# Linear attention into hash-routed experts on one Trainium2 core: k of six batches moved to GpSimd's queue, and a new written order of the first phase

## Chip, core and metric

The kernel runs on one core of a Trainium2 chip. The metric is device time in microseconds. The core has five engines with queues of their own: TensorE (PE, with its weight loads as PEld), VectorE (DVE), ScalarE (ACT), GpSimd (POOL) and SyncE (SP). SP and POOL issue the transfers of this kernel; what they issue is carried by 16 DMA engines.

## What is computed

```python
q_s = exp(q - max(q)) / (sum over head_dim + 1e-9)      # softmax of each row of q
k_s = exp(k - max(k)) / (sum over seq + 1e-9)           # softmax of k along the sequence
kv  = einsum('bhsd,bhse->bhde', k_s, v)                 # 64 x 64 per batch and head
x   = einsum('bhsd,bhde->bhse', q_s, kv)                # as rows: 4608 tokens x 512
expert = token_ids * 2654435761 % 8
out[expert == e] = relu(x[expert == e] @ w1[e]) @ w2[e] # w1 512 x 1024, w2 1024 x 512
```

q, k and v are (8 batches, 8 heads, 576 positions, 64), float32. All 4608 tokens go to one of 8 experts.

## The kernel before

The kernel works in float16 and routes first, so that q is read only in the order in which the experts want it. The index part (L79 to L163) counts where each token goes: an expert has 640 slots, 72 for each of the 8 batches and 64 for tokens beyond 72 of a batch (overflow). Slots are handled in five blocks of 128.

**Names of the steps.** The first phase is cut into named steps, and the list `ORDER` says in which sequence their instructions are issued. Each engine gets its instructions in that sequence (`manual_schedule` covers GpSimd, TensorE, VectorE and ScalarE); between engines semaphores hold. The names:

- V*b*: load v of batch b on POOL's queue, float32 to float16 (L725). k is loaded on SP's queue (L721).
- EK*b*: exp of k on ACT (L324). MK*b*: ones into two columns of v on ACT (L328). KV*b*: 72 matmuls k^T v (L338). SC*b*: division by the sums on DVE (L345 to L351), which gives `kvr` of the batch.
- CNT, OVA, OHA, FND, FDD, QS, ROP, ROD: the overflow tokens. FDD ends with their row numbers `oidx`; ROD ends with the rows of the output.
- G*e*: gather of q rows of expert e, five indirect transfers on POOL (L362). GO: four such for the overflow tokens, which need `oidx`.
- EQ*e_i*: exp of block i on ACT (L373). SM*e*a, SM*e*b: sums over head_dim on DVE (L385 to L387). ML*e*a, ML*e*b: the scaling on DVE (L391). TP*e_i*, TC*e_i*: transposition on TensorE (L403) and its copy. O stands for the overflow tokens.
- PP*e_lo r*, PC*e_lo r*: product of q with `kvr` of the batches from lo on, for head pair r (L414), and its copy into `XT` (L826). XP, XC: the same for the overflow tokens (L437, L801). SH, SD, OV: their distribution over the experts (L447, L453, L811).
- W*e*1, W*e*2: load of w1 or w2 of expert e on POOL's queue in two halves, float32 to float16 (L465).
- A*e_lo_f*, R*e_lo_f*: the first layer, 8 matmuls of 128x288 or 128x352 (L479), and its ReLU on ACT (L484). B*e_i*, C*e_i*, S*e_i*: the second layer, 8 matmuls of 128x512 (L491), its scaling on DVE (L497) and the indirect store on POOL (L501).

`ORDER` covers all batches, the gathers of experts 0 to 4, and both layers of experts 0 and 1. After it a loop over experts 2 to 7 follows (40 blocks of L479 and L491 by turns), into which gathers, weights and products for later experts are placed by position.

**Buffers.** k has three buffers, its exp two, v four, q rows ten, the scaled result four, and each weight one of two pools (even and odd experts). In PSUM there are two buffers of each of three kinds. A load waits until the step that last read its buffer is done: W21 for expert 0's first layer, W12 for nothing.

**Queues.** POOL's transfers count on eight semaphores in turn, so each waits for the landing of the eighth before it. Before `ORDER` starts, SP issues the token numbers and k of batches 0 to 2, and POOL v of batches 0 and 1. Then SP issues k of batch b + 3 as a part of step EK*b*:

```python
def expk(b):
    k16s[b] = at.expk(kraws[b], apool)
    if b + 3 < B_:
        load_k(b + 3)
```

SP does nothing else, so that each k leaves as soon as its buffer is free. On POOL the sequence is, from the built program: v0, v1, v2, G0, v3, v4, GO, W01, v5, G1, v6, v7, W02, W11, W12, G2, G3, first stores of expert 0, W21, G4.

Of the kernel before, what the change touches and what calls it, by code (L numbers as in the profile page):

```python
# [17 lines left out]
B_, H_, S_, DH_ = 8, 8, 576, 64  # L18
# [608 lines left out]


ORDER = """
EK0 MK0 V2 CNT KV0 G0 EK1 OVA SC0 MK1 KV1 OHA EK2 V3 V4 SC1 FND MK2 FDD KV2 EK3 QS GO EQ0_1 ROP SC2 EQ0_0 EQ0_2  # L630
EQ0_3 SM0a EQ0_4 EK4 W01 ROD V5 ML0a G1 SM0b TP0_2 TP0_1 TC0_2 TC0_1 TP0_0 MK3 ML0b TC0_0 KV3 TP0_4 SC3 EK5 V6
TP0_3 V7 W02 TC0_4 MK4 W11 PP0_00 TC0_3 KV4 PC0_00 EQO_0 W12 EQO_1 PP0_01 SC4 EK6 PP0_03 SMOa EQO_3 EQO_2 PC0_01
MLOa PP0_02 G2 PC0_02 SMOb TPO_0 TCO_0 TPO_1 PC0_03 XP0 TCO_1 MLOb A0_0_1 XC0 A0_0_3 R0_0_1 TPO_3 R0_0_3 TPO_2
A0_0_0 MK5 EQ1_0 KV5 EQ1_1 R0_0_0 EQ1_4 EQ1_3 A0_0_2 SC5 EK7 XP1 SM1b MK6 ML1b XC1 KV6 R0_0_2 EQ1_2 MK7 G3 SM1a
TCO_3 KV7 TCO_2 ML1a TP1_3 TP1_4 TC1_3 TC1_4 SC6 TP1_2 TP1_1 TC1_2 SC7 TC1_1 XP2 TP1_0 XC2 PP0_40 XP3 TC1_0
PC0_40 B0_0 XC3 PP1_01 C0_0 PP1_41 SH1 PC1_01 S0_0 PC1_41 PP0_42 SD1 PP1_42 SH0 PC1_42 PC0_42 PP0_43 SD0 PP0_41
B0_1 EQ2_0 PC0_41 OV0 EQ2_1 PC0_43 EQ2_2 PP1_02 C0_1 PP1_00 EQ2_3 A0_288_0 SM2a S0_1 PC1_02 EQ3_1 A0_288_2 EQ3_2
ML2a PC1_00 PP1_03 R0_288_2 PP1_43 R0_288_0 A0_288_1 PC1_43 EQ3_3 PC1_03 TP2_2 EQ3_0 OV1 TP2_0 R0_288_1 TC2_2
A1_0_2 TC2_0 EQ3_4 SM3a A0_288_3 R1_0_2 EQ2_4 PP1_40 W21 A1_0_0 R0_288_3 ML3a TP2_1 PC1_40 G4 B0_2 R1_0_0 TC2_1
SM2b A1_288_3 TP3_1 R1_288_3 C0_2 TP3_0 B0_3 ML2b TC3_1 A1_288_0 C0_3 S0_2 TC3_0 TP2_4 SM3b R1_288_0 S0_3 PP2_03  # L640
B0_4 TC2_4 ML3b PP2_02 W22 A1_288_1 PC2_02 PC2_03 TP3_2 C0_4 R1_288_1 TP2_3 A1_0_1 TC3_2 EQ4_3 S0_4 TC2_3 EQ4_4
PP2_01 TP3_3 EQ4_2 PC2_01 A1_0_3 TC3_3 R1_0_1 PP2_00 TP3_4 R1_0_3 A1_288_2 TC3_4 W31 PC2_00 EQ4_0 PP2_61 PP2_60
R1_288_2 PC2_61 B1_0 EQ4_1 PC2_60 PP2_62 C1_0 PP2_30 PC2_62 B1_2 PC2_30 S1_0 PP2_31 C1_2 PP2_32 B1_3 PC2_31
PC2_32 S1_2 PP2_33 C1_3 PP2_63 B1_1 PC2_33 S1_3 PC2_63 B1_4 C1_1 S1_1 C1_4 S1_4
""".split()


class _Steps:
# [5 lines left out]
    def add(self, name, f, *args):  # L654
        assert name not in self.f, name
        self.f[name] = lambda: f(*args)
# [27 lines left out]
def kernel(  # L684
# [10 lines left out]
    nc = tc.nc  # L695
    V, A = nc.vector.tensor_copy, nc.scalar.copy
    fpool = ctx.enter_context(tc.tile_pool(name="flag", bufs=1))
    with ExitStack() as fctx:
# [17 lines left out]
        with tc.manual_schedule(engines={eng.Pool, eng.PE, eng.DVE, eng.Activation}):  # L716
            kraws, v16s, k16s, pkvs, qs, po, pr, ph, obs, wts, px, pq = ({} for _ in range(12))

            def load_k(b):
                kraws[b] = apool.tile([128, NPAIR * C9 * DH_], F32, tag="kraw", name=f"kraw{b}", bufs=3)  # L720
                nc.sync.dma_start(kraws[b][:], k[b])  # L721

            def load_v(b):
                v16s[b] = apool.tile([128, NPAIR * C9, VW], F16, tag="v16", name=f"v16_{b}", bufs=4)
                nc.gpsimd.dma_start(v16s[b][:].rearrange("p c d -> p (c d)"), v[b])  # L725
# [2 lines left out]
            at.clear()  # L728
            ix = _Index(nc, moe_token_ids, cpool, ipool, ps)
            moe = _Moe(nc, tc, moe_w1, moe_w2, out, ix, ps)  # L730
            for b in range(3):
                load_k(b)
            load_v(0)
            load_v(1)
            ix.consts(tpool)
            ix.core(cpool, lambda: at.fill(ix))

# [4 lines left out]
            add = st.add  # L742
# [6 lines left out]

            def expk(b):  # L750
                k16s[b] = at.expk(kraws[b], apool)
                if b + 3 < B_:
                    load_k(b + 3)

            for b in range(B_):
                if b > 1:
                    add(f"V{b}", load_v, b)
                add(f"EK{b}", expk, b)
                add(f"MK{b}", lambda b: at.mark(v16s[b]), b)
                add(f"KV{b}", lambda b: pkvs.update({b: at.keys(k16s[b], v16s[b])}), b)  # L760
                add(f"SC{b}", lambda b: at.scaled(b, pkvs[b], apool), b)
# [195 lines left out]
```

The softmax here doesn't subtract the row's maximum and nothing guards it: scores larger than these inputs give would overflow.

## Time and profile before

| | |
|---|---|
| time, median of 3 | 239.14 us (238.75 to 239.44) |
| span of the profiled execution (239.44 us) | 237.7 us |
| busy: PE / DVE / ACT / POOL | 196.2 / 138.2 / 113.3 / 116.9 us |
| HBM read / written | 63.25 / 10.49 MB |
| first matmul of expert 0's first layer | 54.6 us |
| start of the loop over experts 2 to 7 | 116.7 us |
| last matmul | 231.4 us |

Times count from the first instruction of the profiled execution. A matmul is pipelined, so PE busy tells that it had work and not how fast it went; for that one divides a group's length by its matmuls. In the chain of waits each step leads to what released the next one, from the start to the last instruction: what stands there with many microseconds was waited for, and by whom is the next line. A group of instructions is given with its line, its output and inputs and its tile sizes.

### The profile page before, as it was taken

To read this page: it belongs to the slowest core of one execution; us is meant where nothing else is said; L and a number is where in the kernel's file an instruction comes from. 1 tells how busy PE (TensorE), PEld (TensorE's weight loads), DVE (VectorE), ACT (ScalarE), POOL (GpSimd) and SP (SyncE) were. 2 spreads that over 40 slices of the span, in tenths; PEclk is the share of its full clock that TensorE was granted. 3 is DMA by queue.
4 is the path that set the end of the run, shared out by engine and by line. 5 is a ranking of instruction groups with operands and counts; after the bars stand their busy time and mean duration, and the time that the engine had idled before them with its cause. 6 is when DMAs were issued, how large, how long until landed. Compare 5 with 4: busy or idle time off the path is not lost.

```text
span 237.7 us, 4865 instructions
## 1 busy us (share of the span) xinstructions
PE 196.2 (83%) x1955; PEld 128.7 (54%) x1955; DVE 138.2 (58%) x260; ACT 113.3 (48%) x175; POOL 116.9 (49%) x140
## 2 busy tenths in 40 slices
PE   3535624629779989999979999999999999999990
PEld 2435623616665556575556476567457656647530
DVE  7995639292592699963387395679358561131140
ACT  8633337764954495284154354555525324405400
POOL 6072332535263545775358788558762254053061
PEclk9999999855955999999999999999999999999996
DMA  6999999999999944969937999997999598832032
GB/s 216 331 311 320 411 337 277 351 227 295 213 215 223 308 165 63 261 168 225 249 112 184 241 228 284 210 243 195 208 226 266 128 204 160 164 133 86 1 130 84
DMA packets 13549, 51.42 MB, mean 216 GB/s; under 512 B 2505, under 2 KB 2505, under 8 KB 12497
## 3 DMA queue, kind: packets, MB, share of 16 engines
q0 software_dynamic: 12224, 41.58, 72.2%
q1 hardware_dynamic: 1296, 9.47, 10.1%
q8 instruction: 17, 0.28, 0.5%
q14 instruction: 12, 0.09, 0.1%
HBM read 63.25 MB, written 10.49 MB: 310 GB/s over the span
## 4 chain that ended last, share of the span: by engine, by line
PE 55%; DMA 24%; DVE 9%; issue 4%; ACT 4%; POOL 2%; POOLq 0%; DVEq 0%; ACTq 0%
PE po L491 24%; PE ph L479 23%; DMA raw<-in_q_dram,gidx 14%; DMA v<-in_v_dram 5%; DMA out_dram<-ob,sidx 4%; PE pq L403 3%; DVE rq L385 2%; ACT k L324 2%; PE px L426 2%; POOL raw L362 2%; PE pt L338 2%; DVE qs L391 1%; DVE A L127 1%; DMA ids<-in_moe_token_ids_dram 1%; ACT qs L373 1%
## 5 line engine op out<-in xcount | busy, mean ns | idle before, releaser
L479 PE MATMUL ph<-XT,w1r 128*128 128x320 f16 (+2 forms) x512 | 76.0, 304 | 0.4 <-ACT hT L484 0.4
L491 PE MATMUL po<-w2r,hT 128*128 128x512 f16 x320 | 74.3, 384 | 0.0
L484 ACT ACTIVATE hT<-ph 128x640 f16<-128x640 f32 (+2 forms) x64 | 44.9, 704 | 51.1 <-PE ph L479 50.8
L501 POOL DMA_INDIRECT out_dram<-ob,sidx x40 | 40.8, 1020 | 56.4 <-DVE ob L497 51.6
L497 DVE TENSOR_SCALAR ob<-po 128x512 f32<-128x512 f32 x40 | 27.6, 690 | 62.4 <-PE po L491 54.9
L362 POOL DMA_INDIRECT raw<-in_q_dram,gidx x40 | 46.7, 1169 | 30.6 <-DVE row L162 6.6
L479 PEld LDWEIGHTS <-w1r 128*128 128x128 f16 x512 | 50.0, 100 | 21.1 <-issue 0.9
L491 PEld LDWEIGHTS <-hT 128*128 128x128 f16 x320 | 30.9, 99 | 34.0 <-issue 1.8
L373 ACT ACTIVATE qs<-raw 128x512 f16<-128x512 f32 (+1 forms) x44 | 26.0, 625 | 17.3 <-DMA raw<-in_q_dram,gidx 17.1
L385 DVE TENSOR_REDUCE rq<-qs 128x16 f32<-128x1024 f16 (+1 forms) x18 | 26.1, 1450 | 4.4 <-ACT qs L373 4.3
L403 PE MATMUL pq<-ident,qs 128*128 128x128 f16 (+1 forms) x176 | 16.7, 237 | 12.0 <-DVE qs L391 11.0
L391 DVE TENSOR_TENSOR qs<-qs,rq 128x1024 f16<-128x1024 f16 (+1 forms) x18 | 26.2, 1455 | 0.3
L338 PE MATMUL pt<-v,k 64*64 64x65 f16 x576 | 15.4, 226 | 10.3 <-ACT v L328 8.9
L403 PEld LDWEIGHTS <-qs 128*128 128x128 f16 (+1 forms) x176 | 12.7, 108 | 16.6 <-issue 9.7
L338 PEld LDWEIGHTS <-k 64*64 64x64 f16 x576 | 15.0, 139 | 10.9 <-issue 10.4
L324 ACT ACTIVATE k<-kraw 128x2304 f16<-128x2304 f32 x8 | 16.9, 2118 | 1.9 <-PE pt L338 1.5
L465 POOL DMA_DIRECT2D w1r<-in_moe_w_dram x16 | 9.3, 580 | 9.1 <-PE px L414 6.1
L414 PE MATMUL px<-qT,kvr 128*128 128x72 f16 (+1 forms) x96 | 8.0, 215 | 5.4 <-DVE XT L826 3.0
L414 PEld LDWEIGHTS <-kvr 128*128 128x128 f16 x96 | 6.3, 103 | 8.5 <-issue 6.0
L877 ACT CAST XT<-px 128x864 f16<-128x864 f32 (+1 forms) x6 | 4.8, 799 | 11.9 <-PE px L426 11.9
L465 POOL DMA_DIRECT2D w2r<-in_moe_w_dram x16 | 9.4, 594 | 2.1 <-DMA v<-in_v_dram 1.6
L345 DVE TENSOR_SCALAR rec<-pt 128x4 f32<-128x4 f32 x8 | 1.3, 162 | 15.2 <-PE pt L338 15.1
(106 smaller groups left out, 136.4 us busy)
## 6 DMA issues: line engine op xcount, KB each, us to landing
kraw<-in_k_dram SPq DMA_DIRECT2D x8, 1152.0 KB, 10.3
w1r<-in_moe_w_dram POOLq DMA_DIRECT2D x16, 512.0 KB, 8.5
w2r<-in_moe_w_dram POOLq DMA_DIRECT2D x16, 512.0 KB, 8.5
v<-in_v_dram POOLq DMA_DIRECT2D x8, 594.0 KB, 16.3
raw<-in_q_dram,gidx POOLq DMA_INDIRECT x40, 6.2
out_dram<-ob,sidx POOLq DMA_INDIRECT x40, 6.8
raw<-in_q_dram,oidx POOLq DMA_INDIRECT x4, 15.5
ids<-in_moe_token_ids_dram SPq DMA_DIRECT2D x1, 36.0 KB, 1.9
```

What stands on the lines that cost most here:

```text
L324: self.nc.scalar.activation(k16[:].rearrange("p c d -> p (c d)"), kraw[:], ACT.Exp)
L338: nc.tensor.matmul(pkv[s, r, 0:DH_ + 1], lhsT=k16[s, r * C9 + c, :], rhs=v16[s, r * C9 + c, 0:DH_ + 1], start=(c == 0), stop=(c == C9 - 1))
L362: nc.gpsimd.indirect_dma_start(out=raw[0:w, :], out_offset=None, in_=self.q[:, :], in_offset=bass.IndirectOffsetOnAxis(ap=idx[0:w, i:i + 1 ...
L373: self.nc.scalar.activation(q16[0:w, i].rearrange("p h d -> p (h d)"), raws[i][0:w, :], ACT.Exp)
L385: nc.vector.reduce_sum(rv, qv, axis=AX.X)
L391: nc.vector.tensor_tensor(out=qf, in0=qf, in1=rv.rearrange("p i h -> p (i h)").unsqueeze(2) .to_broadcast([w, (hi - lo) * H_, DH_]), op=AL ...
L403: nc.tensor.transpose(pv[:, r, o:o + w[j]], q16[0:w[j], j, 2 * r:2 * r + 2, :] .rearrange("p h d -> p (h d)"), self.ident[0:w[j], 0:w[j]])
L479: nc.tensor.matmul(ph[:, i, :hi - lo], lhsT=w1r[:, dc, fc * 128:(fc + 1) * 128], rhs=XTp[:, e % 2, dc, lo:hi], start=(dc == 0), stop=(dc = ...
L484: self.nc.scalar.activation(hT[:, 2 * f2:2 * f2 + 2, lo:hi], ph[:, :, :hi - lo], ACT.Relu)
L491: nc.tensor.matmul(po[:], lhsT=hT[:, fc, blk * 128:(blk + 1) * 128], rhs=w2r[:, fc, :], start=(fc == 0), stop=(fc == FC - 1))
L497: self.nc.vector.tensor_scalar(out=ob[:], in0=po[:], scalar1=1.0 / SX, scalar2=None, op0=ALU.mult)
L501: sc = self.nc.gpsimd.indirect_dma_start(out=self.out[:, :], out_offset=bass.IndirectOffsetOnAxis(ap=self.ix.sidx[:, e, blk:blk + 1], axis=0),
```

## The change

k of batches 0 and 1 stay on SP. k of batch 2 is issued on POOL after v0 and v1, and k of batches 3 to 7 become steps K3 to K7 of `ORDER`, on POOL too. `ORDER` is replaced as a whole: the same steps in another sequence. POOL's transfers are then, from the built program: v0, v1, k2, G0, k3, G1, v2, v5, GO, k4, v3, v4, k6, k5, v6, k7, v7, G2, W01, G4, W11, G3, W02, W21, W12, six stores, W31, W22. On TensorE, expert 0's first layer (A0) comes after the last KV and after the overflow's SH, where it stood between them before; A0, A1, B0 and B1 follow one another with TP2, TP3 and PP2 among them. The loop over experts 2 to 7 is as it was.

```diff
             def load_k(b):
                 kraws[b] = apool.tile([128, NPAIR * C9 * DH_], F32, tag="kraw", name=f"kraw{b}", bufs=3)
-                nc.sync.dma_start(kraws[b][:], k[b])
+                (nc.sync if b < 2 else nc.gpsimd).dma_start(kraws[b][:], k[b])
...
-            for b in range(3):
+            for b in range(2):
                 load_k(b)
-            load_v(0)
-            load_v(1)
+            for b in range(2):
+                load_v(b)
+            load_k(2)
...
             def expk(b):
                 k16s[b] = at.expk(kraws[b], apool)
-                if b + 3 < B_:
-                    load_k(b + 3)

             for b in range(B_):
                 if b > 1:
                     add(f"V{b}", load_v, b)
+                if b > 2:
+                    add(f"K{b}", load_k, b)
```

`ORDER` before, up to the first layer of expert 1, and after, up to the second layer of expert 0:

```diff
-EK0 MK0 V2 CNT KV0 G0 EK1 OVA SC0 MK1 KV1 OHA EK2 V3 V4 SC1 FND MK2 FDD KV2 EK3 QS GO EQ0_1 ROP SC2 EQ0_0 EQ0_2
-EQ0_3 SM0a EQ0_4 EK4 W01 ROD V5 ML0a G1 SM0b TP0_2 TP0_1 TC0_2 TC0_1 TP0_0 MK3 ML0b TC0_0 KV3 TP0_4 SC3 EK5 V6
-TP0_3 V7 W02 TC0_4 MK4 W11 PP0_00 TC0_3 KV4 PC0_00 EQO_0 W12 EQO_1 PP0_01 SC4 EK6 PP0_03 SMOa EQO_3 EQO_2 PC0_01
-MLOa PP0_02 G2 PC0_02 SMOb TPO_0 TCO_0 TPO_1 PC0_03 XP0 TCO_1 MLOb A0_0_1 XC0 A0_0_3 R0_0_1 TPO_3 R0_0_3 TPO_2
-A0_0_0 MK5 EQ1_0 KV5 EQ1_1 R0_0_0 EQ1_4 EQ1_3 A0_0_2 SC5 EK7 XP1 SM1b MK6 ML1b XC1 KV6 R0_0_2 EQ1_2 MK7 G3 SM1a
-TCO_3 KV7 TCO_2 ML1a TP1_3 TP1_4 TC1_3 TC1_4 SC6 TP1_2 TP1_1 TC1_2 SC7 TC1_1 XP2 TP1_0 XC2 PP0_40 XP3 TC1_0
...
+EK0 CNT G0 EK1 MK0 OVA KV0 MK1 KV1 SC0 K3 OHA G1 EK2 SC1 FND EQ0_0 EQ0_3 EQ0_1 EQ0_2 FDD EQ0_4 SM0a EK3 V2 V5 GO
+QS EQ1_0 EQ1_2 ML0a ROP EQ1_4 EQ1_3 SM0b EQ1_1 TP0_0 TP0_2 TC0_0 TC0_2 TP0_1 ROD MK2 K4 TC0_1 KV2 ML0b V3 V4
+SM1a K6 MK5 TP0_4 TP0_3 TC0_4 K5 EQO_0 V6 EQO_1 ML1a EQO_2 TC0_3 EQO_3 SMOa TP1_0 TP1_2 TC1_0 TC1_2 TP1_1 EK4
+SMOb MLOa TC1_1 K7 MK3 MLOb TPO_0 KV3 TCO_0 SM1b TPO_2 V7 TPO_1 TCO_2 MK4 G2 SC3 TPO_3 TCO_1 TCO_3 ML1b XP0 XC0
+SC2 TP1_3 KV4 TC1_3 PP1_01 PP0_01 SC4 EK6 XP1 PC0_01 W01 PC1_01 PP0_03 XC1 PC0_03 PP1_00 G4 EK5 PP1_02 PC1_02
+KV5 PC1_00 MK6 KV6 SC5 EK7 PP0_00 PP1_03 SC6 XP2 W11 PC0_00 PC1_03 MK7 PP0_02 XC2 KV7 PC0_02 TP1_4 SC7 EQ2_0
+EQ2_4 PP0_43 EQ2_2 XP3 PC0_43 XC3 PP0_42 EQ2_1 SH0 PC0_42 SM2a EQ2_3 TC1_4 PP0_41 G3 SH1 PC0_41 SD0 PP1_41
+PP0_40 SD1 A0_0_0 ML2a PC0_40 A0_0_3 R0_0_0 PP1_43 A0_0_1 R0_0_3 OV0 PC1_43 A0_0_2 R0_0_1 OV1 W02 PP1_40 SM2b
...
```

More of the change, by code (lines that the diff above doesn't have):

```diff
@@ L635 @@
-TCO_3 KV7 TCO_2 ML1a TP1_3 TP1_4 TC1_3 TC1_4 SC6 TP1_2 TP1_1 TC1_2 SC7 TC1_1 XP2 TP1_0 XC2 PP0_40 XP3 TC1_0
[L636 to L644, printed above, removed]
+EK0 CNT G0 EK1 MK0 OVA KV0 MK1 KV1 SC0 K3 OHA G1 EK2 SC1 FND EQ0_0 EQ0_3 EQ0_1 EQ0_2 FDD EQ0_4 SM0a EK3 V2 V5 GO
@@ new lines @@
+EQ2_4 PP0_43 EQ2_2 XP3 PC0_43 XC3 PP0_42 EQ2_1 SH0 PC0_42 SM2a EQ2_3 TC1_4 PP0_41 G3 SH1 PC0_41 SD0 PP1_41
+PP0_40 SD1 A0_0_0 ML2a PC0_40 A0_0_3 R0_0_0 PP1_43 A0_0_1 R0_0_3 OV0 PC1_43 A0_0_2 R0_0_1 OV1 W02 PP1_40 SM2b
+A0_288_3 R0_0_2 PC1_40 A0_288_2 R0_288_3 PC1_41 ML2b EQ3_0 TP2_1 A1_0_2 R0_288_2 TC2_1 TP2_3 EQ3_2 A1_0_3 TC2_3
+R1_0_2 PP1_42 TP2_4 EQ3_1 A0_288_0 TC2_4 R1_0_3 SM3a PC1_42 TP2_0 A0_288_1 R0_288_0 EQ3_3 A1_288_2 W21 TC2_0
+R0_288_1 ML3a TP2_2 EQ3_4 B0_3 W12 EQ4_2 EQ4_0 SM3b TP3_2 EQ4_1 B0_1 EQ4_3 TC3_2 EQ4_4 ML3b TP3_1 R1_288_2
@@ L645 @@
+A1_288_1 TC3_1 C0_1 TP3_3 R1_288_1 A1_288_3 TC3_3 S0_1 C0_3 B0_2 TC2_2 R1_288_3 S0_3 PP2_30 C0_2 PP2_32 PC2_30
+B0_0 PC2_32 S0_2 PP2_33 C0_0 PP2_31 A1_0_0 PC2_33 S0_0 PC2_31 A1_0_1 R1_0_0 TP3_0 TP3_4 R1_0_1 TC3_0 B0_4 TC3_4
+PP2_02 C0_4 PP2_62 PC2_02 B1_0 PC2_62 S0_4 PP2_01 C1_0 PP2_00 A1_288_0 PC2_00 PC2_01 S1_0 PP2_61 PP2_03 R1_288_0
+PC2_61 B1_1 W31 PC2_03 W22 B1_2 C1_1 S1_1 B1_4 C1_2 S1_2 B1_3 C1_4 S1_4 PP2_60 PP2_63 C1_3 PC2_60 PC2_63 S1_3
 """.split()
```

## The prediction

> **What bounds the kernel now.** I read the busy slices first, then a table of busy time by stage, then the chain of waits, and last the timelines of TensorE and GpSimd around the places that the chain names.
>
> The slices: each digit is the busy tenth of 5.94 us.
> ```profile
> PE   3535624629779989999979999999999999999990
> PEclk9999999855955999999999999999999999999996
> DMA  6999999999999944969937999997999598832032
> ...
> HBM read 63.25 MB, written 10.49 MB: 310 GB/s over the span
> ```
> DMA is full in the first 14 slices (83 us) while TensorE has holes; then TensorE is full and DMA has holes. So there are two phases, and only the first has time to give. The stage table (stage, its length, busy of PE, PEld, DVE, ACT, POOL, then granted clock, DMA share, GB/s landed) puts numbers on it:
> ```profile
> 0.00:54.00 54.00, 23.87 (x567) 21.77 (x567) 37.09 (x102) 30.89 (x40) 22.01 (x40) 0.92 0.99 310
> 54.00:88.20 34.20, 30.54 (x409) 20.27 (x409) 20.41 (x38) 21.85 (x42) 15.90 (x19) 0.77 0.97 241
> 88.20:116.70 28.50, 28.45 (x213) 17.56 (x213) 20.65 (x38) 13.54 (x25) 17.11 (x18) 1.00 0.79 174
> ...
> 116.70:231.40 114.70, 113.29 (x769) 69.10 (x767) 59.34 (x84) 47.05 (x69) 60.70 (x64) 1.00 0.75 183
> ```
> From 88.2 us TensorE idles 1.5 us in all; the loop over experts 2 to 7 (from 116.7) is 114.7 us of matmuls. The loop is not edited. So the question is when the loop starts.
>
> The chain, before the dense part (start, length, what):
> ```profile
> 16.99 19.84 DMA raw<-in_q_dram,gidx
> ...
> 53.55 10.94 DMA v<-in_v_dram
> ...
> 67.69 14.12 DMA raw<-in_q_dram,gidx
> ...
> 89.00 2.17 PE ph L479 x16
> ```
> Three transfers that stood behind others in a full DMA. TensorE itself (start, length, group, idle before):
> ```profile
> 54.61 4.02 PE L479 MATMUL ph<-XT,w1r 128*128 128x288 f16 x16
> ...
> 60.39 1.34 PE L338 MATMUL pt<-v,k 64*64 64x65 f16 x72
> 61.67 1.15 PE L479 MATMUL ph<-XT,w1r 128*128 128x288 f16 x8
> ...
> 64.39 1.34 PE L338 MATMUL pt<-v,k 64*64 64x65 f16 x72 [1.22 <-ACT v L328]
> 66.08 2.14 PE L338 MATMUL pt<-v,k 64*64 64x65 f16 x72 [0.35 <-ACT v L328]
> ...
> 88.83 2.34 PE L479 MATMUL ph<-XT,w1r 128*128 128x288 f16 x16
> ```
> Expert 0 starts at 54.6, before batches 5 to 7 have arrived, and crawls among them: 251 ns per matmul at 54.6, 146 ns at 88.8. The last batches come at 64 to 66 because W01, G1 and, on SP, all of k share the DMA with v.
>
> **What the Trainium skill says.** "DMA: Bandwidth & Descriptors", section "Issuing engines are not separate DMA queues": transfers of SP, ACT and GpSimd run on the same 16 engines. The trace agrees: the DMA share is 1.03 at 20 to 40 us with both queues and 1.03 at 60 to 83 us, after the last k, with GpSimd's alone. Moving k there buys order, not bandwidth. The same page, "Queues, rings and completion order": an engine takes packets from its queues in turn. The trace agrees that two queues delay each other: of the loads issued at the start the quickest k lands in 5.3 us, no v in under 10.9. "TensorE: Matmul & The Clock Gate", section "What's actually happening": an idle array runs at half clock until some 3.4 us of sustained work. The pairs above (251 and 146 ns; 2.14 and 1.34 us) agree. The granted-clock row says 9 before 44 us, yet a batch of L338 takes 2.19 us there; I go by the durations.
>
> **The change, part by part.** Bytes are from the tile shapes at 4 bytes read per element: k 1.18 MB a batch, v 1.217, a gather of five (G) 1.18, GO 1.05, half an expert's weights (W) 2.10. For the whole kernel they give 9.44 + 9.73 + 10.49 + 33.55 = 63.2 MB, the page's 63.25. By the landing of the last v (53.55 + 10.94 = 64.5) all k and v, G0, G1, GO and W01 had been read in queue order, 24.7 MB in 62.5 us from 2.0: **395 GB/s**.
>
> *The order of transfers.* After: k0, k1, v0, v1, k2, G0, k3, G1, v2, v5, GO, k4, v3, v4, k6, k5, v6, k7, v7, G2, W01, G4, W11, G3, W02, W21, W12. Up to v7 this is 22.6 MB: 57.2 us of DMA. A gap must be added. Gathers follow each other every 1.3 us (13.05, 14.39, 15.69, 16.99), 0.262 MB each, 202 GB/s, half the rate; before, SP's k filled the other half. G1 is issued at about 19 to 26 with a backlog that ends near 23, and v2 follows: 2 us lost, bounds 0 (backlog covers it) and 8 (all nine gathers of G1 and GO at half rate, 11.7 us for 5.6 us of data, 6.1, and 2 for GO waiting for its indices). So v7 lands at 2.0 + 57.2 + 2 = 61.2, W01 at 69.5, W11 at 77.8, W02 at 86.
>
> *k on GpSimd's queue* adds six DMA issues of 0.57 us (the v row), 3.4 us, while GpSimd was busy 38 of 88 us: hidden. Behind a waiting k now stand v and gathers. k7 waits for EK4 on ACT, EK4 for TP1 and so for ML1a. VectorE's work up to ML1a ends at about 37 by its rows; k7 is issued near 42, when DMA has transfers queued to 55: nothing. v7 waits for KV3, which stands behind TPO_0 and MLOa (about 42): issued at 45, nothing. GO waits for the overflow indices (25.2 before; about 24 after, since v1 comes earlier), queue position 27: nothing. W21 waits for expert 0's first layer, with W12 behind it; W02 is still moving then.
>
> *The chain after v7.* MK7 0.3, KV7 2.1 (cold), SC7 1.25 (0.16 + 0.18 + 0.86 and gaps): 64.9. TensorE then has two overflow products and shares (16 matmuls of L447: 3.5 us warm, 216 ns as in L491; 6.7 cold, as the eight of L491 at 73.5 us took 3.35) and five small groups, 1.0 to 1.8 us: A0_0_0 starts at 69.4 (warm) to 73.4 (cold). W01 lands at 69.5, no later than that. I take the middle, **71.4**; A0 starts 17 us later than now.
>
> *From there to the loop*, by warm rows of the chain: A0 and A1 are each 4 x 0.98 + 4 x 1.19 = 8.7 us; B0 and B1 5 x 1.73 = 8.65; TP2 and TP3 ten of 0.22, 2.2; PP2 4 x (0.19 + 0.19 + 0.13), 2.0; three PP1 of 0.13, 0.4. Sum 39.3 us. Before, 62 us pass from the first A0 block to the loop. Waits: W11 at 77.8 is needed at about 79, W02 at 86 at about 86, W12 near 97 at about 102. For those two, and 1.7 of lost clock at half odds, I add 1.9. In these 41 us ACT has 16 ReLUs of 0.7, ten exponentials of 0.6 and some ten evictions of 0.45, 22 us; VectorE two softmaxes of 6.8 (1.75, 1.76, 1.21, 1.21 and the small ones) and ten each of 0.42, 0.69 and 0.5, 30 us: hidden. The loop starts at 71.4 + 39.3 + 1.9 = 112.6 instead of 116.7: **4.1 us earlier**. Everything behind it is the same instructions. The sum is against the profiled span of 237.7; that execution took 239.44, the three 238.75 to 239.44. I take the difference off the median: 239.14 - 4.1 = 235.0.
>
> **Rivals.**
> *Warm and full (229).* DMA runs at 416 GB/s without a gap (33.3 MB from 2 to 83 us, less than the waits allow) and TensorE stays warm: W01 at 64.2 sets A0, W02 at 80 makes B0 wait 2, loop at 64.2 + 39.3 + 2 + 1 = 106.5, 10 us gained. For it: the stretch before v7 has TensorE work for most of its time. Against it: the cold rows up to 54 us at a similar load.
> *Gathers starve the queue (slower, 241).* Place: G1 and GO, 19 to 33 us. Price: 8 us of DMA instead of 2; v7 and A0 6 us later, loop at 118.6, +1.9: 241.0. It decides from 4 us above my 2. For it: the 1.3 us spacing. Against it: k3, v2 and v5 stand among the gathers.
> *Given back (239).* The loop starts earlier, but W22, issued only after B1_0, lands late: A0 to B1_0 is 30 us, so issue near 104, landing near 115 with W31; it is needed at 112.6 + 8.7 = 121. Against it: 6 us of slack.
>
> **How the numbers follow.** A measurement of this kernel tells about 0.3% from no change. Likeliest 0.50 (232 to 238); warm and full 0.22; starved 0.20; given back 0.08. The own range of the likeliest takes A0 at 69.4 to 73.4 and waits of 1 to 3. The range 228.5 to 240.5 takes in the second case and most of the third. Faster: 0.50 + 0.22 and 0.02 of the fourth, 0.74. Same: 0.05 of the fourth and 0.03 of the third, 0.08. Slower: 0.18.
>
> **What would show it.** Right: DMA at 9 until about 90 us; MK7 near 61; first L479 matmul at 69 to 74 and no hole over 1 us after it; the loop near 113. Warm: L447 at 216 ns, not 420. Starved: a DMA slice under 9 between 19 and 35 us. Given back: PE waiting on L491 for w2r at 121. Wrong altogether: the loop starting at 117 or later with v7 landed by 61.

## The result, and the profile after

| | before | after |
|---|---|---|
| time, median of 4 runs | 239.08 us (238.75 to 239.44) | 235.27 us (234.83 to 235.74) |
| span of the profiled execution | 237.7 us | 234.0 us |
| MK7, the first step that needs v7 | 65.8 us | 63.7 us |
| first matmul of expert 0's first layer (A0) | 54.6 us | 74.2 us |
| start of the loop over experts 2 to 7 | 116.7 us | 114.0 us |
| last matmul | 231.4 us | 228.0 us |

The ratio is 0.984, with a 95% interval of 0.982 to 0.987. The forecast was 235.0 us. Later runs of the same kernel on another chip gave another sign; they stand under the experiments and belong to the result. Runs far above the fastest of their kernel count as slow, and every ratio given compares fast runs alone while the medians are of all runs, so that the two can differ (1.029 against 1.022 in after_again) and in before_ob6 even point opposite ways (1.004 against 0.992).

The busy slices of the kernel after, each digit 5.85 us:

```profile
PE   3554345383789999999999999999989999999990
PEclk9998555587668999999999999999999999999998
DMA  6999899999999989946999999998999598832032
...
HBM read 63.25 MB, written 10.49 MB: 315 GB/s over the span
```

DMA holds 8 or more from the second slice to the 17th (6 to 99 us); the 8 in slice 5 (23 to 29 us) stands where the gathers of G1 and GO are issued. TensorE is full from slice 13 (70 us).

The table of stages (start and end, length, busy of PE, PEld, DVE, ACT and POOL, granted clock, DMA share, GB/s landed), the first three rows for the stages shown of before, the last for the loop:

```profile
0.00:54.00 54.00, 26.45 (x599) 23.15 (x600) 44.83 (x110) 34.70 (x51) 31.71 (x48) 0.75 0.96 293
54.00:88.20 34.20, 29.02 (x418) 20.95 (x418) 19.86 (x41) 22.62 (x40) 16.59 (x21) 0.80 0.98 256
88.20:116.70 28.50, 28.50 (x193) 16.64 (x192) 16.48 (x29) 10.60 (x19) 13.70 (x17) 1.00 0.84 179
114.00:228.00 114.00, 113.29 (x771) 69.19 (x768) 59.76 (x85) 47.34 (x70) 60.88 (x64) 1.00 0.80 191
```

VectorE's busy time up to 54 us rose from 37.1 to 44.8 us and ACT's from 30.9 to 34.7: softmaxes and copies have moved in front, into time in which TensorE waited for k and v anyway. TensorE's busy time in the loop stands at 113.29 us in both kernels.

The chain of waits of the kernel after (start, length, what):

```profile
48.37 15.32 DMA v<-in_v_dram
...
64.50 1.53 PE pt L338 x71
...
68.57 3.41 PE pr L447 x8
72.23 1.86 PE pr L447 x8
...
75.47 1.14 PE ph L479 x8
```

No gather and no weights stand between v7 and expert 0 any more. TensorE in the same place, and at the start of the loop (start, length, group, idle before):

```profile
64.50 1.49 PE L338 MATMUL pt<-v,k 64*64 64x65 f16 x72 [0.92 <-ACT xov L802]
...
68.38 3.61 PE L447 MATMUL pr<-Q,xov 128*128 128x512 f16 x8
...
72.03 2.04 PE L447 MATMUL pr<-Q,xov 128*128 128x512 f16 x8
...
74.17 1.15 PE L479 MATMUL ph<-XT,w1r 128*128 128x288 f16 x8
...
113.97 6.68 PE L479 MATMUL ph<-XT,w1r 128*128 128x320 f16 x48
```

A0 starts at 74.17 at full speed (1.15 us for 8; before it took 4.02 for 16) and from there to the loop 39.8 us pass, with 0.2 us of waits in all. So 2.7 us of the 3.7 us of span came before the loop. Of the other 1.0 us, 0.7 came inside the loop (114.7 to 114.0 us) and 0.3 behind the last matmul; the prediction had costed both as equal. Before, VectorE (first line) waited 4.09 us for a store to free one of the four result buffers, its next softmax came late, and TensorE (second line) waited 1.33 us for that:

```profile
119.92 0.69 DVE L497 TENSOR_SCALAR ob<-po 128x512 f32<-128x512 f32 x1 [4.09 <-DMA out_dram<-ob,sidx]
```

```profile
124.67 0.62 PE L403 MATMUL pq<-ident,qs 128*128 128x128 f16 x8 [1.33 <-DVE qs L391]
```

In the kernel after both waits are gone; its loop has other waits of 0.6 us in all. Whether the four buffers are the reason is the question of the run before_ob6 below.

GpSimd's queue after, at the two places of which the prediction had said "nothing":

```profile
44.98 0.53 POOL L721 DMA_DIRECT2D kraw<-in_k_dram  x1 [5.61 <-ACT k L324]
48.37 0.53 POOL L725 DMA_DIRECT2D v<-in_v_dram  x1 [2.85 <-PE pt L338]
```

GpSimd waits 5.6 and 2.9 us, while the DMA share from 40 to 64 us is 1.03: the DMA never ran short, and the waits cost nothing that shows, as forecast.

### The profile page after: what moved, and what is told of

It is laid out like the page before. It is cut to its first block, busy times and chain, and to the rows that moved or that the text cites. A ratio compares the mean times of both kernels' runs of the same rounds, so it can differ in the third digit from the quotient of the medians.

```text
span 234.0 us, 4848 instructions
## 1 busy us (share of the span) xinstructions
PE 194.6 (83%) x1955; PEld 128.0 (55%) x1955; DVE 139.0 (59%) x260; ACT 113.9 (49%) x175; POOL 122.5 (52%) x146
## 4 chain that ended last, share of the span: by engine, by line
PE 48%; DMA 24%; POOL 10%; issue 9%; DVE 5%; ACT 2%; POOLq 1%; ACTq 0%; DVEq 0%
PE ph L479 21%; PE po L491 19%; DMA v<-in_v_dram 14%; POOL raw L362 6%; DMA out_dram<-ob,sidx 6%; DMA raw<-in_q_dram,gidx 4%; PE pr L447 2%; POOL out_dram L501 2%; PE pq L403 2%; PE pt L338 2%; PE px L414 1%; DVE A L127 1%; POOL w1r L465 1%; PE px L426 1%; ACT hT L484 1%
## 5 line engine op out<-in xcount | busy, mean ns | idle before, releaser
L479 PE MATMUL ph<-XT,w1r 128*128 128x320 f16 (+2 forms) x512 | 74.1, 299 | 0.9 <-ACT hT L484 0.6
L501 POOL DMA_INDIRECT out_dram<-ob,sidx x40 | 40.2, 1005 | 62.1 <-DVE ob L497 57.6
L491 PE MATMUL po<-w2r,hT 128*128 128x512 f16 x320 | 72.5, 379 | 0.0
L479 PEld LDWEIGHTS <-w1r 128*128 128x128 f16 x512 | 49.1, 98 | 20.1 <-issue 1.4
L362 POOL DMA_INDIRECT raw<-in_q_dram,gidx x40 | 47.7, 1193 | 23.7 <-issue 7.9
L491 PEld LDWEIGHTS <-hT 128*128 128x128 f16 x320 | 30.7, 98 | 33.5
L373 ACT ACTIVATE qs<-raw 128x512 f16<-128x512 f32 (+1 forms) x44 | 26.2, 623 | 18.3 <-DMA raw<-in_q_dram,gidx 17.8
L338 PE MATMUL pt<-v,k 64*64 64x65 f16 x576 | 15.3, 228 | 8.9 <-ACT v L328 5.7
L338 PEld LDWEIGHTS <-k 64*64 64x64 f16 x576 | 15.0, 142 | 9.4 <-issue 4.1
L827 ACT CAST XT<-px 128x288 f16<-128x288 f32 (+1 forms) x14 | 5.7, 431 | 11.0 <-PE px L414 11.0
```

Of the source, the lines that this page charges most:

```text
L338: nc.tensor.matmul(pkv[s, r, 0:DH_ + 1], lhsT=k16[s, r * C9 + c, :], rhs=v16[s, r * C9 + c, 0:DH_ + 1], start=(c == 0), stop=(c == C9 - 1))
L362: nc.gpsimd.indirect_dma_start(out=raw[0:w, :], out_offset=None, in_=self.q[:, :], in_offset=bass.IndirectOffsetOnAxis(ap=idx[0:w, i:i + 1 ...
L373: self.nc.scalar.activation(q16[0:w, i].rearrange("p h d -> p (h d)"), raws[i][0:w, :], ACT.Exp)
L479: nc.tensor.matmul(ph[:, i, :hi - lo], lhsT=w1r[:, dc, fc * 128:(fc + 1) * 128], rhs=XTp[:, e % 2, dc, lo:hi], start=(dc == 0), stop=(dc = ...
L491: nc.tensor.matmul(po[:], lhsT=hT[:, fc, blk * 128:(blk + 1) * 128], rhs=w2r[:, fc, :], start=(fc == 0), stop=(fc == FC - 1))
L501: sc = self.nc.gpsimd.indirect_dma_start(out=self.out[:, :], out_offset=bass.IndirectOffsetOnAxis(ap=self.ix.sidx[:, e, blk:blk + 1], axis=0),
```

## The experiments

Each job ran its kernels and the kernel before by turns on one chip. The expectations of the first four runs were made from the two profiles above. Neither of these contains what every later profile of a kernel with indirect gathers does: holes in TensorE's work for which no wait is shown. So a table of the runs with the new steps comes first. "Holes" is TensorE's idle time without a wait ("issue"); KV1 is its end; GO the issue of its first gather; times in us, from one profiled execution each.

| kernel | holes | KV1 | GO | DMA share 20 to 40 us | A0 | span | span - A0 | ratio to before |
|---|---|---|---|---|---|---|---|---|
| after, first comparison | 0 | 18.1 | 28.3 | 0.96 | 74.2 | 234.0 | 159.8 | 0.984 [0.982, 0.987] |
| k_on_sp | 9.7 | 27.2 | 32.3 | 1.03 | 85.4 | 245.3 | 159.9 | 1.017 [1.009, 1.026] |
| w01_early | 11.3 | 28.0 | 33.8 | 0.77 | 88.9 | 248.7 | 159.8 | none; 251.17 and 242.15 |
| v2_before_g1 | 12.0 | 23.8 | 29.2 | 0.94 | 82.6 | 241.9 | 159.3 | 1.013 [1.008, 1.018] |
| w01_before_g2 | 8.1 | 27.8 | 33.6 | 0.78 | 82.2 | 242.2 | 160.0 | 1.011 [1.005, 1.016] |
| warm | 14.1 | 27.8 | 33.8 | 0.78 | 88.7 | 248.2 | 159.5 | 1.033 [1.027, 1.038] |
| best | 6.2 | 23.8 | 29.5 | 0.94 | 78.6 | 238.6 | 160.0 | 0.993 [0.990, 0.997] |
| after_again | 11.8 | 27.5 | 33.6 | 0.79 | 83.5 | 243.1 | 159.6 | 1.029 [1.018, 1.041] |
| best_g1_late | 10.5 | 21.3 | 26.3 | 1.02 | 92.9 | 251.7 | 158.8 | 1.050 [1.044, 1.056] |
| plain_g | 0 | 18.0 | 26.4 | 1.02 | 70.4 | 230.9 | 160.5 | 0.963 [0.956, 0.969] |

In w01_early the two medians stand for a ratio that was not given. With the holes, the times of seven runs (k_on_sp, new_dma_old_steps, w01_early, v2_before_g1, w01_before_g2, warm and best) lie above every range that had been set down for them; what they can tell is which steps moved, and not what a move is worth without holes. Two things are to be seen. Span minus A0 is 158.8 to 160.5 us in every kernel with the new steps, with holes or without: what happens before A0 sets the end, and nothing behind it gives anything back. And KV1's end, the first place with holes, lies between 18 and 28 us in kernels with the same steps.

### The change in parts

**k back on SP**, the new order kept:

```diff
-                (nc.sync if b < 2 else nc.gpsimd).dma_start(kraws[b][:], k[b])
+                nc.sync.dma_start(kraws[b][:], k[b])
```

> The changed kernel with every k back on SP's queue (the new order of steps kept; SP issues a k as soon as its buffer is free). Order theory (the gain comes from the sequence in which data arrive and from the steps that follow it; the queue is only the carrier): k3 to k5 now run ahead of G0, v1 and v2, DMA does not starve at 20 to 28 us, v7 lands within 2 us of the changed kernel's 63.7: 234.5 to 237 us. Queue theory (taking k off the queue that competes with v is the gain): back to 238.5 to 240 us.

246.71 us against 242.15 of before in the same job. The DMA share from 20 to 40 us is 1.03 where after_again has 0.79, so a second queue does fill what GpSimd's leaves open. Yet MK7 runs at 74.0 us: v7 was issued only at 53.9 us, after 11.4 us of waiting for a KV step, and took 20 us from there. So the full DMA did not bring v7 earlier, and neither theory's time came. With 9.7 us of holes in the run, what k's place is worth without them is not shown.

**k on GpSimd's queue, the old order of steps** (K3 to K7 right behind EK0 to EK4 in the old `ORDER`):

```diff
-EK0 MK0 V2 CNT KV0 G0 EK1 OVA SC0 MK1 KV1 OHA EK2 V3 V4 SC1
+EK0 K3 MK0 V2 CNT KV0 G0 EK1 K4 OVA SC0 MK1 KV1 OHA EK2 K5 V3 V4 SC1
```

> The old order of steps, with k of batches 2 to 7 on GpSimd's queue, each issued where SP issued it (K3 after EK0, and so on to K7 after EK4). Order theory: no gain, 238.5 to 242 us, since GpSimd then waits for the EK steps in the middle of its queue and the weights still stand ahead of the last v. Queue theory: 235 to 236.5 us.

241.47 us, ratio 0.997 [0.994, 1.000], within the order theory's range. With 6.9 us of holes in its profile (of an execution of 243.19 us), the move of k by itself brings at most 0.6%. A0 starts at 57.1 us at half speed (16 matmuls in 4.02 us), as before.

**The new order of transfers, the old order of steps:**

```diff
-EK0 MK0 V2 CNT KV0 G0 EK1 OVA SC0 MK1 KV1 OHA EK2 V3 V4 SC1
+EK0 MK0 CNT G0 K3 G1 V2 V5 KV0 EK1 OVA SC0 MK1 KV1 OHA EK2 SC1
...
```

> GpSimd's transfers in the new sequence up to v7 (then W01, G2, W02, W11, G3, W12, W21), all other steps in the old order. Order theory: both belong together; A0_0 stands ahead of KV5 to KV7 on TensorE and waits for W01, which now lands near 68 us, so KV7 ends near 75 us: 243 to 250 us. A theory that the sequence of transfers alone makes the gain expects 235 to 236.5; one that the steps alone make it expects 238.5 to 240 us, as before.

267.14 us, ratio 1.102 [1.092, 1.111]: the slowest of all. The old steps ask for the gathers of expert 0, then v3 and v4, then expert 0's weights; the new transfers bring G1, v2 and v5 first. TensorE's three slices from 40 to 60 us have the busy digits 1, 2 and 2, it has 11.4 us of holes besides, and A0, at 75.3 us, again runs at half speed. The order theory had the direction and 243 to 250 us. So the new transfers without the new steps cost 10%, holes included, and k's move without either brought next to nothing; the new steps with the old transfers were not run.

### Where the transfers stand

The next versions move one or two names of the new order; each line shows where the name comes in, and it goes out at its old place.

```diff
 w01_early:
-ROP EQ1_4 EQ1_3 SM0b EQ1_1 TP0_0 TP0_2 TC0_0 TC0_2 TP0_1 ROD MK2 K4 TC0_1
+ROP EQ1_4 EQ1_3 SM0b EQ1_1 TP0_0 TP0_2 TC0_0 TC0_2 TP0_1 ROD MK2 W01 K4 TC0_1
 v2_before_g1:
-SC0 K3 OHA G1 EK2
+SC0 K3 OHA V2 G1 EK2
 w01_before_g2:
-TPO_1 TCO_2 MK4 G2 SC3
+TPO_1 TCO_2 MK4 W01 G2 SC3
```

> The changed kernel with W01 issued before k4 and not after G2. Order theory: 2.1 MB go ahead of k4 to v7, which land 5 us later (v7 near 68.8), and the chain from v7 to A0 is the same 10.5 us: A0 near 79, loop 4 to 5 us later: 238.5 to 240.5 us. Rival (the place of the weights is indifferent, since DMA has holes later): 235 to 236 us.

251.17 us. 2.10 MB ahead of k4 are 5.3 us at the prediction's 395 GB/s. A0 stands at 88.9 us where after_again, on another chip, has 83.5, 5.4 later; that the two figures are so near is luck, since MK7 is 8.9 later (77.5 against 68.6) and the holes lie in other places. With W01 ahead of k4 in the queue, A0 still comes 11.4 us after MK7: v7 and not W01 is what A0 waits for in this run. The rival, that the weights' place is indifferent, finds no support.

> The changed kernel with v2 issued before the five gathers of G1 and not after them. Starvation theory (DMA shares of 0.84 and 0.78 at 24 to 28 us are the gathers' issue rate, and what is lost there comes back as a later v7): the two shares rise to 0.95 or more, v7 lands 0.8 to 1.5 us earlier, time 233.8 to 234.8 us. Rival (v7's landing is set by something behind it, or the steps can't use an earlier v7): 235.0 to 235.6, as the changed kernel.

245.18 us, ratio 1.013 [1.008, 1.018]. With v2 queued ahead of the gathers, the DMA share from 20 to 40 us is 0.94 and GO leaves at 29.2 us. But KV4 and KV6 ran under the gathers of G2 and G4 and lost there more than had been won: MK7 came at 71.6 us.

> The changed kernel with W01 issued before the gathers of G2. If A0 waits for W01: W01 lands some 3 us earlier and A0 starts earlier by what it waited. My reading is that A0 (74.2) waits for TensorE's own chain after v7 and W01 lands just before (near 73): no change in time, 235.0 to 235.7. Rival (W01 sets A0): 233 to 234.5 us.

244.46 us, ratio 1.011 [1.005, 1.016]. A0 did not gain: between MK7 (68.3) and A0 (82.2) pass 13.9 us, where the kernel after has 10.5. TensorE stands 3.0 us in SH0, for a reason that is plainer in best, below.

**warm** adds 11 matmuls of 128x512, whose results nobody reads, ahead of and behind KV7, so that SH0 runs at full clock; **best** puts this and the two moves together:

```diff
-SC6 XP2 W11 PC0_00 PC1_03 MK7 PP0_02 XC2 KV7 PC0_02 TP1_4 SC7
+SC6 XP2 WM0 W11 PC0_00 PC1_03 MK7 PP0_02 XC2 WM1 KV7 PC0_02 TP1_4 WM2 SC7
```

> The changed kernel with 11 matmuls of 128x512 added in TensorE's gaps between 62 and 67 us; nothing reads their results. Clock theory (SH runs at half clock because TensorE idled 1.8 us at 63 to 65.5): SH's first eight matmuls take 1.9 us and not 3.6, A0 starts 1 to 2 us earlier unless W01 holds it: 234.0 to 235.0 us. Rival (the added matmuls only delay KV7, or W01 holds A0): 235.2 to 236.5 us.

250.24 us. The two SH take 1.89 us each, 3.8 together, where the kernel after took 5.65: the mechanism works and is worth 1.9 us of SH. What that does to the total is not shown; the run has 14.1 us of holes.

> The three together (v2 before G1, W01 before G2, the added matmuls). If the chain v7, KV7, SC7, SH, A0 is what sets the start of the dense part, the gains add: A0 near 71, 232.0 to 233.8 us. If another limit stands close behind (DVE's sums, W11, the later weights): 234 to 235.5 us.

240.05 us, ratio 0.993 [0.990, 0.997] on a chip on which the other three were slower than before. In the later jobs it had the fewest holes of the kernels with indirect gathers and the new steps, 6.2 us. Whether it also beats the kernel after where there are no holes was not measured.

Its profile shows a cost that the expectation left out. v7 was in time (MK7 at 63.1 us, 0.6 earlier than in the kernel after), yet A0 came 15.5 us later instead of 10.5, and 3.7 us of that is one wait. W01 now stands ahead of G2 in the queue, and ACT waits for G2's rows in EQ2 (first two lines). XC3, the copy of the last overflow product, stands behind these exponentials in ACT's written order, and SH0 waits for it (third line):

```profile
68.38 0.63 ACT L373 ACTIVATE qs<-raw 128x512 f16<-128x512 f32 x1 [4.03 <-DMA raw<-in_q_dram,gidx]
72.05 1.15 ACT L373 ACTIVATE qs<-raw 64x512 f16<-64x512 f32 x2 [3.04 <-DMA raw<-in_q_dram,gidx]
...
73.72 1.25 PE L447 MATMUL pr<-Q,xov 128*128 128x512 f16 x5 [3.69 <-ACT xov L802]
```

After the stop the second SH runs cold again (3.50 us), so the added matmuls were lost too. Neither the kernel after nor warm, with W01 behind G2, has this wait in SH0. A version with XC3 ahead of EQ2 was not run.

### The same kernel again, and the buffers

> The changed kernel itself, once more, beside the kernel before on the same chip, with a profile. The runs so far have holes in TensorE's KV steps, 6 to 14 us, that the profile puts down to 'issue' (no wait), and all of them while GpSimd issues gathers; the first profile of the changed kernel has none. If the holes belong to the chip or to its moment, and not to the edits of those runs: this run has them too wherever the chip has them, 6 to 10 us of holes, 239 to 244 us beside a kernel before at 240 to 245. If they come from the edits: no holes and 0.98 of the kernel before, 235 us.

The kernel after, without any edit: 248.12 us against 242.72, ratio 1.029 [1.018, 1.041]. The kernel before had grown too, by 3.6 us over the first comparison. It has 11.8 us of holes, and so the chip's or the moment's side of the expectation holds, with a time above its range. TensorE in KV0 and KV1, first of the kernel after in the first comparison, then of this run:

```profile
14.19 3.96 PE L338 MATMUL pt<-v,k 64*64 64x65 f16 x144 [3.13 <-ACT v L328]
```

```profile
14.51 1.57 PE L338 MATMUL pt<-v,k 64*64 64x65 f16 x45 [3.44 <-ACT v L328]
16.51 0.39 PE L338 MATMUL pt<-v,k 64*64 64x65 f16 x6 [0.43 <-issue]
...
19.43 0.34 PE L338 MATMUL pt<-v,k 64*64 64x65 f16 x5 [0.41 <-issue]
20.17 0.36 PE L338 MATMUL pt<-v,k 64*64 64x65 f16 x5 [0.40 <-issue]
20.90 0.32 PE L338 MATMUL pt<-v,k 64*64 64x65 f16 x4 [0.37 <-issue]
...
25.92 1.62 PE L338 MATMUL pt<-v,k 64*64 64x65 f16 x51 [1.07 <-issue]
30.01 2.08 PE L242 MATMUL po<-Z,AO 64*64 64x2 f16 x72 [2.46 <-DVE AO L230]
```

and GpSimd in the same time:

```profile
11.61 1.08 POOL L362 DMA_INDIRECT raw<-in_q_dram,gidx  x1 [6.53 <-DVE row L162]
...
24.03 0.94 POOL L362 DMA_INDIRECT raw<-in_q_dram,gidx  x1 [0.30 <-issue]
24.97 1.20 POOL L725 DMA_DIRECT2D v<-in_v_dram  x2
33.55 1.06 POOL L362 DMA_INDIRECT raw<-in_q_dram,oidx  x1 [7.38 <-ACT qs L373]
```

After the first 45 come bursts of one to six matmuls, mostly four to six, then nothing for 0.4 us (at times 1.1), a burst every 0.74 us: so it goes on until 25, when the last gather of G1 has been issued, and then, from 25.9, 51 matmuls run without a break. The 144 matmuls that took 3.96 us in the first profile take 13 here. What follows from it is a chain: KV1 late, FND late (it starts at 30.0 instead of 20.8), the overflow indices late, and GO, which stands in GpSimd's only queue with k4, v3 and v4 behind it, waits 7.4 us. DMA runs dry:

```profile
PE   2543349275755999999999999999999999999980
...
DMA  6999965999999990993799999998999687932032
```

Slices 6 and 7 (30 to 43 us) hold 6 and 5. Further patches come at 57 us, where KV4 meets G2, and at 70 us, where KV7 meets G4. In this same run KV5 and KV6, without a gather beside them, take 3.71 us for 144 matmuls without a hole.

The other kernel of this job is the one before with six result buffers, to see the wait of 4.09 us:

```diff
-        opool = P("o", 4)
+        opool = P("o", 6)
```

> The kernel before with six buffers for the scaled result and not four. In the kernel before VectorE waits at 119.9 us for a store of 9.9 us, and TensorE stands 1.33 us for it at 123.3; the changed kernel has no such stop. If that stop is the loop's share of the gain: 0.993 to 0.996 of the kernel before (1 to 1.6 us). If TensorE's stop is made up elsewhere: 1.000. The profile also tells whether the kernel before has the holes on this chip: if they belong to the chip, some 3 to 7 us of them in the KV steps under gathers.

240.80 us, ratio 1.004 [0.999, 1.009]. VectorE's wait for a store is gone, and from the loop's start (119.6) to the end pass 119.4 us instead of 121.0 (120.0 in the kernel after): the wait for a buffer was what cost this time. But the first phase of the run ended 2.9 us later than in the profile of before, and in the total nothing shows. It also gives the nearest look at the kernel before with holes: 2.6 us, where the new order has 6 to 14. In the old order, KV0 lies under G0 and breaks up; KV1 comes after G0's last gather and does not; KV2, beside GO, has one gap of 0.4 us.

### What makes the holes

Two theories. Gathers: GpSimd, issuing indirect gathers, keeps TensorE from getting on. Chip: some chips have such holes in steps of many small matmuls, whoever issues. The test takes the indirect form out of G0 to G4 and leaves engine, queue, buffers and bytes. It leaves out the routing of the q rows:

```diff
+            if plain is not None:
+                r0 = plain * 576 + len(raws) * 128
+                nc.gpsimd.dma_start(raw[0:w, :], self.q[r0:r0 + w, :])
+                raws.append(raw)
+                continue
             nc.gpsimd.indirect_dma_start(
...
-                add(f"G{e}", lambda e: qs.update({e: gather(e)}), e)
+                add(f"G{e}", lambda e: qs.update({e: gather(e, plain=e)}), e)
```

> The changed kernel with the indirect gathers of G0 to G4 replaced by plain loads of as many rows of q at fixed places (same buffers, same bytes, same engine and queue; the four of GO stay indirect). It leaves the routing of q rows out, so its rows are not those the experts want. Gathers' theory: TensorE's holes without a wait, found in KV0 and KV1 of the repeated changed kernel (KV1 ended at 27.5 us there, at 18.1 in the first profile), come from GpSimd issuing indirect gathers. Then KV0 and KV1 run unbroken here and end by 19 us, holes without a wait sum to under 2 us, GO is issued by 28 us, A0 starts at 72 to 75 us, and the time is 0.97 to 0.985 of the kernel before on the same chip. Chip's theory: the holes belong to the chip or the moment and to steps of many small matmuls, whoever issues transfers. Then KV0 and KV1 show them as before, 6 to 12 us in all, and the time is 1.01 or more of the kernel before.

232.71 us against 242.29, ratio 0.963 [0.956, 0.969]. TensorE (line numbers are 5 higher behind the edit):

```profile
13.83 4.17 PE L338 MATMUL pt<-v,k 64*64 64x65 f16 x144 [2.98 <-ACT v L328]
...
60.73 1.34 PE L338 MATMUL pt<-v,k 64*64 64x65 f16 x72 [0.67 <-ACT xov L807]
...
70.42 1.15 PE L484 MATMUL ph<-XT,w1r 128*128 128x288 f16 x8
```

No hole at all, on a chip on which the kernel of the next paragraph, run in the same job, has 10.5 us of them. So the holes need the gathers' issue; the chip's theory alone is out. Which part of the issue it is, the indirect form or its length (1.0 us of GpSimd against 0.54), was not separated. A0, at 70.4 us, and the ratio came out lower than even the gathers' theory had them (72 to 75 us, 0.97 to 0.985).

The other traces say the same within a run. In the 11 later kernels with indirect gathers, 24 of the 88 KV steps have no gather issued beside them, and none of these has more than 0.25 us between the starts of two matmuls; of the other 64, 45 have. Beside large matmuls the gathers and stores do no such thing in after_again: GpSimd issues 40 indirect stores and 15 gathers behind 85 us, under blocks of L479 and L491, and TensorE has no hole there.

But the gathers are not enough either: the first profile has the same gathers over the same KV0 and KV1 and no hole. What the second condition is, chip or moment, stays open.

The time of plain_g is below the clean run of the kernel after too, by 3.1 us of span. There the gathers' other cost is seen, the rate at which they are issued. The stretch from 20 to 28 us, of the kernel after and then of this one (the last two numbers are DMA share and GB/s):

```profile
20.00:28.00 8.00, 2.94 (x83) 2.60 (x84) 6.43 (x18) 4.83 (x7) 6.77 (x7) 0.57 0.88 297
```

```profile
20.00:28.00 8.00, 2.83 (x89) 2.49 (x90) 6.25 (x18) 5.11 (x8) 3.43 (x6) 0.59 1.00 327
```

**G1 behind GO.** The last run takes best and moves the gathers away from KV1:

```diff
-SC0 K3 OHA V2 G1 EK2 SC1 FND EQ0_0 EQ0_3 EQ0_1 EQ0_2 FDD EQ0_4 SM0a EK3 V5 GO QS EQ1_0 EQ1_2 ML0a
+SC0 K3 OHA V2 EK2 SC1 FND EQ0_0 EQ0_3 EQ0_1 EQ0_2 FDD EQ0_4 SM0a EK3 V5 K4 V3 V4 GO G1 QS ML0a
...
-EQO_0 V6 EQO_1 ML1a EQO_2 TC0_3 EQO_3 SMOa TP1_0
+EQO_0 V6 EQO_1 EQO_2 TC0_3 EQO_3 SMOa EQ1_0 EQ1_2 EQ1_1 EQ1_4 EQ1_3 SM1a ML1a TP1_0
```

> The version with v2 ahead of G1, W01 ahead of G2 and 11 added matmuls, and G1 moved on behind k4, v3, v4 and GO, so that no gather is issued between G0 and GO; the exponentials of expert 1's rows and their sums stand accordingly later. If KV1 under G1's gathers and the late GO are what the changed kernel loses on these chips: KV1 ends by 23 us, FND by 26 us, GO is issued by 29 us, no DMA slice under 9 between 18 and 40 us, A0 starts at 73 to 77 us, time 0.98 to 0.99 of the kernel before. If the loss lies elsewhere (KV4 and KV7 under G2 and G4): the version without this move took 0.993 of the kernel before, and this one takes the same or more.

253.72 us, ratio 1.050 [1.044, 1.056]. The first half came as expected: KV1 ended at 21.3, FND at 25.4, GO left at 26.3, and the DMA share from 20 to 40 us was 1.02. The second half, A0 at 73 to 77 us and 0.98 to 0.99, was a miss, and the edit itself made it. G1's rows now arrive near 45 us; TP1 waits for them, and EK4 stands behind TP1's copies in the written order of ACT. TensorE is idle for 13.0 us ahead of TP1 (slices 7 and 8 of it, 38 to 50 us, hold 0), and k7 needs EK4:

```profile
54.58 0.53 POOL L721 DMA_DIRECT2D kraw<-in_k_dram  x1 [9.50 <-ACT k L324]
57.69 0.53 POOL L725 DMA_DIRECT2D v<-in_v_dram  x1 [2.58 <-issue]
```

In the kernel after the same wait was 5.6 us, with the DMA full behind it; here k7 leaves 9.6 us later than there, v7 at 57.7, and G2 and G4 follow at once (59.6 to 72.3 us), over KV4 and the products, with most of the 10.5 us of holes. So freeing KV1 worked, and moving G1 behind everything cost more than that gave. A version that keeps EK4 ahead of TP1 was not tried.

## Why the prediction was right, and where not

**The bound.** "When the loop starts" is what decides, and the runs show it more sharply than the prediction put it: in ten profiles with the new steps the end lies 158.8 to 160.5 us behind A0, while A0 itself moves from 70.4 to 92.9.

**The order of transfers** was the step with an error of size. v7 was to land at 61.2: 2.0 of start, 57.2 of data, 2 lost to the gathers' rate. MK7 could run at 63.7, so that term measured 4.5 instead of 2 (bounds were 0 and 8) if the 395 GB/s hold. With the gathers of G0 to G4 plain, MK7 ran at 59.95, 3.8 earlier, though on another chip: this points to the gathers' issue for most of the 4.5 us. Of this, 1.0 us is seen directly as 0.88 instead of 1.00 of 8 us; where the rest lies among the transfers was not settled.

**k on GpSimd's queue.** Costed at nothing, and nothing it cost: k7 was issued at 45.0 (forecast near 42), v7 at 48.4 (45), with DMA full. k's move alone measured 0.997 [0.994, 1.000]. That both are safe holds only as long as the waits stay inside the backlog; best_g1_late shows the other side.

**The chain after v7.** MK7, KV7 and SC7 took 3.6 us (3.7), in part by luck: KV7 took 1.49 us and not the cold 2.1, and had stood 0.5 us behind MK7 for a copy on ACT. From SC7's end at 67.34 to A0 6.8 us passed, near the middle (6.5) between warm (4.5) and cold (8.5) that had been taken: SH0 ran cold, 3.61, SH1 nearly warm, 2.04. The Trainium skill, "TensorE: Matmul & The Clock Gate", section "What's actually happening", has the array come to full speed after some 3.4 us of sustained work; SH0's 3.61 us followed by an SH at 255 ns a matmul agrees, and so do the 1.89 us of both SH behind the added matmuls. A0 came at 74.2 instead of 71.4, nearly all of it v7's 2.5.

**From there to the loop** 41.2 us were forecast, 39.8 measured. The sum of warm rows, 39.3, was right; of the 1.9 for waits and clock only some 0.5 came, 0.2 of it as waits. **The loop** and the end behind it, costed as equal, gave 1.0 us. The three errors, +2.8, -1.4 and -1.0, left +0.4 us of the profiled span (233.6 forecast, 234.0 measured): that the time came out closer than its steps did is luck.

**The rivals.** Warm and full did not come: its sign was L447 at 216 ns, and SH0 ran at 451 ns a matmul. (Its rate of 416 GB/s is 411 by its own 33.3 MB from 2 to 83 us; nothing hangs on it.) Given back did not come either: TensorE waited for no w2r. Gathers starve the queue came in part: its sign, a DMA slice under 9 between 19 and 35 us, is there once in the first comparison, and the term at 4.5 us lies 2.5 above the 2 taken, below the 4 above it from which this rival decides. In after_again DMA starved close to the place that it had named (19 to 33 us there, 30 to 43 here), but less by the issue rate of the gathers than by GO, waiting 7.4 us at the head of the queue for indices that TensorE had made late; the prediction had put that wait at nothing, and at 2 us in this rival's bound. Its price, 6 us on A0 and 241, was too low as well: A0 at 83.5, 248 us.

**What the prediction did not contain** is the step from which that comes. It took a KV step as 2.2 us cold and 1.34 warm, whatever GpSimd did, because the one profile shown had no other. The change moved KV0 and KV1 under ten gathers issued one after the other, and hung the one queue on their end through FND, FDD and GO. The trace of before could not show that this costs anything, and in the first comparison it did not. So the forecast holds for the comparison that it was made for; for this kernel in general the verdict depends, as far as these runs go, on whether the holes come: 0.984 without, 1.029 with them.

## What to carry to other kernels

When all transfers stand in one queue, look at each waiting issue for what is behind it and for how long the backlog lasts: 5.6 us of waiting were free at 45 us, 7.4 us at 26 us let the DMA run dry, in a run that ended 9 us later. Plan dense steps of small matmuls away from stretches in which GpSimd issues indirect gathers, the chain to such a queue's next wait above all, and look at what the move delays: taking W01 ahead of G2, or G1 behind GO, made an engine's written order wait for the rows that now came later. And a result of 1.6% wants a second chip before it is believed.

## What was not expected of the hardware

In all four jobs behind the first comparison, on four chips, TensorE stops without a wait in steps of small matmuls while GpSimd issues indirect gathers: mostly 4 to 6 matmuls of L338, then 0.4 us (at times 1.1) of nothing, every 0.74 us. The holes come to 6 to 14 us in all with the new steps, 11.4 with the new transfers alone, and 2.6 and 6.9 in the two kernels with the old order of both. With plain loads of the same bytes in G0 to G4 there were none. In broken KV steps the first burst is often 45 to 55 matmuls long. That would fit instructions running short, and the Trainium skill, "Runtime: NRT & Kernel Launch", section "Instruction fetch mechanics", has each engine's instructions fetched by DMA in blocks, mostly hidden. The traces have such packets (17 of 16 KB in one queue of after_again), but they do not bear the thought out: the only ones between 16 and 33 us of after_again start at 17.8 and 18.4 us and last 0.3 and 1.1 us, while the bursts go on until 25.9. What stops TensorE, and why the first comparison was spared, stays open.

The kernel before itself measured 238.75 to 239.44 in the first comparison and 237.67 to 248.23 in the later jobs.
